# Two more head pairs on the all-fp32 attention path: 40 tiles in place of 32

## The chip, the cores and the metric

The kernel runs on one core of one Trainium2 chip. The metric is the time of one execution on the device in microseconds (us), and the time of the kernel before is the median of three runs. The engines are TensorE (PE in the profile, with its weight loads as PEld), VectorE (DVE), ScalarE (ACT), GpSimd (POOL) and SyncE (SP), which here only issues DMAs. Each takes its instructions in the order of its own program and waits where an operand is not there yet.

## The reference

Attention with a position bias for 4 batches, 8 heads, 576 positions and head dimension 64, then a two-layer network with a gate on the 2304 rows of 512 that come out of it.

```python
scores = scale * np.matmul(q, k.transpose(0, 1, 3, 2))
x = (psi_rel / psi_i)[..., None]                # log1p of distances, over log1p of the row
bias = np.maximum(x @ w1 + b1, 0.0) @ w2        # 32 hidden units, one output per head
scores = scores + bias.transpose(2, 0, 1)[None]
scores = scores - np.max(scores, axis=-1, keepdims=True)
attn = np.exp(scores)
attn = attn / (np.sum(attn, axis=-1, keepdims=True) + 1e-09)
out = np.matmul(attn, v)                        # then [B*S, 512]
h = out @ w_in                                  # 512 -> 2048, weights float64
g = h * np.clip(h + 3.0, 0.0, 6.0) / 6.0
return g @ w_out                                # 2048 -> 512, weights float64
```

## The kernel before

Heads go in pairs (4 to a batch), since two heads of 64 fill 128 partitions. A *unit* is a batch, a head pair and a part of the query rows: part 0 is rows 0 to 255 in four tiles of 128 rows (two row blocks by two heads), part 1 is rows 256 to 575 in five. All 16 units of part 0 come first, batch after batch (units 0 to 15, tiles 0 to 63), then the 16 of part 1. The function `direct` says which units take the direct path; before, those are units 0 to 7, the first two batches.

The direct path of a unit of part 0: the scores of a tile are fp32 products (`qk_step`, L523); DVE adds the bias and finds the maximum (`soft_max`, L555); ACT takes the exponential with the row sum (`soft_exp`, L566); TensorE transposes the tile in five fp32 pieces (`soft_low`, L614) and ACT copies them out of PSUM (L617); `pv_first` multiplies by V in fp32 (L656) and spreads the reciprocals of the row sums over the partitions with four small products (L667); `x_first` scales and splits the result into two fp16 parts (L679 and L685 on ACT, L683 on DVE, L686 on POOL). Since the scaling by the row sum comes last, a tile has no normalisation of its own.

The split path of all other units: q and k are split into a high and a low part (ACT L402, POOL L409), the scores are three products (L543), each tile is normalised by small DVE instructions (L574, L578), split into two fp16 parts (L123 on ACT or L117 on POOL, then L140 on DVE) and transposed by a DMA from SP's queue (L631). V is split too (L123, L140, two small DMAs L452 and L453). The product with V is 28 fp16 matmuls (L698); `x_high` and `x_low` (L712, L140) take the result out.

The network works on a batch part at a time. `ffn` makes `h_ps` (L773), runs ACT L763, DVE L756, ACT L750 and POOL L752 on it, then makes `o_ps` (L796). The weights come as float64 and are converted on the chip: `w_in_prep` and `w_out_prep` take their bit patterns apart on ACT (L256), POOL (L257) and DVE (L264, L267, L270) and split them (L123, L140). At the end of `w_out_prep` the largest power of two over all rows is found by `row_ratio`: a DVE reduction into `m_w` (L146), a TensorE transpose of it (L152), a DVE reduction into `g_w` (L154) and a TensorE product (L156) that spreads the number. Only then can the waiting `g` tiles of batch 0 be scaled (ACT L123, DVE L121) and the first `o_ps` begin.

The bias table is made once in 36 groups of 16 rows (`z_group` on DVE L838 and ACT L842, `bias_mm` on TensorE L855 as 8 matmuls, `bias_out` on ACT L871), stored to DRAM and loaded for each tile pair (L484).

The main loop runs over the tile number n: front(n) takes tile n's maximum, tile n-2's transposes or split, the unit of tile n-5's product with V. Until tile 45 (`open_steady`) a scheduler may reorder instructions on all engines but keeps the data flow; PSUM then holds three double banks for scores, transposes and bias groups (tag `s`) and two single banks for `h_ps`, `o_ps`, `pv_ps` and `m_ps` (tag `w`). From tile 45 on TensorE's order is that of the text, with two double and four single banks.

Of the kernel before, what the change touches and what calls it, by code (L numbers as in the profile page):

```python
# [10 lines left out]
F32 = mybir.dt.float32  # L11
# [4 lines left out]
ALU = mybir.AluOpType  # L16
# [5 lines left out]
PAIRS = H // 2  # L22
# [2 lines left out]
NG = S // 16  # L25
CQ = 2.0 ** -25
VC = 5 * 128
CFG = {'z0': 'AD', 'gz': 12, 'z1': 'AD', 'gz2': 16, 'zeng': 'DDA', 'sg': 'P', 'wm1': 'A', 'wm2': 'RRAAAAAA', 'hl': 'AP', 'gl': 'PP', 'vm': 'A', 'g0': 8, 'rwi': 2.0, 'rw0': 0.3, 'rw1': 0.7, 'ro': 0.85, 'rb': 1.7, 'rf0': 1.3, 'rf': 2.0, 'rf1': 1.55, 'la': 6, 'gq': 2, 'gap': 0.0, 'wu': 8, 'act': 'o', 'g1': 2, 'w64': 5, 'rfo': 2.3, 'tv': 'A', 'pw': 0, 'po': 0, 'gr': 'AD', 'wb': 3, 'fb': 2, 'spn': 45, 'sw': 45, 'ws': 2, 'kn': 10, 'kw': 1, 'os': 11, 'ro2': 2.0, 'bo': 12, 'rb0': 1.5}
F64_BIAS = 2.0 ** -112
F64_MAX = float(np.uint32(0x0FEFFFFF).view(np.float32))  # L30

# [2 lines left out]
def attention_moe_kernel(  # L34
# [16 lines left out]
    nc = tc.nc  # L51
    cfg = CFG
    tc.cur_priority = 10000
    B = qk.shape[0]
    DM, DFF = w_in.shape
    KC = DM // 128
    KF = DFF // 128

    const = ctx.enter_context(tc.tile_pool(name="const", bufs=1))
# [38 lines left out]

    open_psum(stack_p, 3, 2)
    eye_sb = const.tile([128, 128], F32, name="eye_sb")  # L100
    r_sb = const.tile([128, 2, 2 * PAIRS * 4], F32, name="r_sb")
    wi = big.tile([128, 2, KC, DFF], F16, name="wi")
    wo = big.tile([128, 2, KF, DM], F16, name="wo")
    bias_d = [dr_p.tile([H, min(128, S - i), S], F32, name=f"bias{i}") for i in range(0, S, 128)]
# [5 lines left out]
    pscale = {}  # L110
# [270 lines left out]
    def load_direct(b, p):  # L381

        t = qk_p.tile([128, 512 + S], F32, tag="hi", name="qk0")
        with behind():
            dq("q").dma_start(out=t, in_=qkd[b, p])
        qk_t[b, p, 0] = t
# [5 lines left out]
    def load_qk(b, p, u):  # L392
        w = S + QW[u]
        t = st_p.tile([128, 1024], F32, tag="st", name="st")[:, 0:w]
        with behind():
            dq("k").dma_start(out=t, in_=qk[b, p][:, 256 * u:256 * u + w])
        st_t[b, p, u] = t

    def split_qk_a(b, p, u):
        w = S + QW[u]  # L400
        hi = qk_p.tile([128, 512 + S], F32R, tag="hi", name="qkh")[:, 0:w]
        nc.scalar.activation(out=hi, in_=st_t[b, p, u], func=AF.Copy)  # L402
        qk_t[b, p, u] = hi

    def split_qk_b(b, p, u):
        t, hi = st_t[b, p, u], qk_t[b, p, u]
        lo = qk_p.tile([128, 512 + S], F32R, tag="hi", name="qkl")[:, 0:S + QW[u]]
        for c, w in ((KC0[u], S), (QC0[u], QW[u])):
            nc.gpsimd.tensor_sub(  # L409
                out=lo[:, c:c + w], in0=t[:, c:c + w], in1=hi[:, c:c + w].bitcast(F32)  # L410
            )
        qk_t[b, p, u] = (hi, lo)
# [17 lines left out]
    def load_v(b, p, u):  # L430
        if (b, p, u) in v_t:
            return
        if direct(b, p, 4 * u):
            t = v_p.tile([128, VC], F32, tag="vh", name="vf")
        else:
            t = st_p.tile([128, VC], F32, tag="vs", bufs=2, name="vs")
        with behind():
            dq("v").dma_start(out=t, in_=vp[b, p])
        v_t[b, p, u] = t
# [53 lines left out]
    units = [(b, p, u) for u in range(2) for b in range(B) for p in range(PAIRS)]  # L493
# [148 lines left out]
    def x_tile(b, u):  # L642
        if (b, u) not in x_t:
            x_t[b, u] = x_p.tile([128, 2, KC, QW[u]], F16, tag="x", name="x")
        return x_t[b, u]
# [3 lines left out]
    def pv_first(b, p):  # L649
# [20 lines left out]
            )  # L670
        pv_t[b, p, 0] = ps

    def x_first(b, p):
        ps = pv_t.pop((b, p, 0))
        n = 256
        x = x_tile(b, 0)
        xr = hl_p.tile([128, 2, n], F32, tag="hl", name="xr")
        xs, rb = xr[:, 0], xr[:, 1]
        nc.scalar.activation(  # L679
            out=rb, in_=ps[:, 1, 0:n], func=AF.Copy,  # L680
            scale=pscale["x1"][:, p:p + 1] if b else pscale["v0"][1],
        )
        nc.vector.tensor_mul(out=xs, in0=ps[:, 0, 0:n], in1=rb)  # L683
        xh = x[:, 0, p]
        nc.scalar.activation(out=xh, in_=xs, func=AF.Copy)  # L685
        nc.gpsimd.tensor_sub(out=x[:, 1, p], in0=xs, in1=xh)  # L686
# [279 lines left out]
    def aux(n):  # L966
        b, p, t = tiles[n]
        k = unit_no[n]
        l = t - UT[int(t >= 4)][0]
        if l == 0 and PAIRS <= k + 2 < len(units):  # L970
            b2, p2, u2 = units[k + 2]
            if direct(b2, p2, 4 * u2):
                load_direct(b2, p2)
            else:
                load_qk(b2, p2, u2)
        if k + 1 < len(units) and not direct(units[k + 1][0], 0, 4 * units[k + 1][2]):
            if l == 1:
                split_qk_a(*units[k + 1])
            if l == 2:
                split_qk_b(*units[k + 1])  # L980
            if l == 3:
                split_qk_c(*units[k + 1])
        if l == 0 and k < 13:
            load_v(*units[k])
        if l == 1 and 13 <= k + 1 < len(units):
            load_v(*units[k + 1])
        if not direct(b, p, t):
            if l == 2:
                split_v_a(*units[k])
            if l == 3:  # L990
                split_v_b(*units[k])
        if b + 1 < B and t < 4 and p >= 1:
            if b + 1 not in vgen:
                vgen[b + 1] = v_scale(b + 1)
            next(vgen[b + 1], None)
# [28 lines left out]
    for cs in (slice(512, LT), slice(0, 512)):  # L1024
        nc.vector.tensor_scalar(
            out=T[:, cs], in0=T[:, cs], scalar1=w1_sb, scalar2=None, op0=ALU.mult
# [25 lines left out]
    def drain(gen):  # L1052
        for _ in gen:
            pass
# [34 lines left out]
    def open_ffn():  # L1089
        nonlocal phase  # L1090
        drain(gen_w)
        hidden_scale(0)
        for c in range(KC):
            xv = x_t[0, 0][:, :, c]
            nc.vector.tensor_scalar(
                out=xv, in0=xv, scalar1=pscale["r1"][:, c:c + 1], scalar2=None, op0=ALU.mult
            )
        if cfg["fb"] > 1:
            x1 = const.tile([128, KC], F32, name="x1")
            nc.vector.tensor_scalar(  # L1100
                out=x1, in0=pscale["r1"], scalar1=pscale["v1"][1], scalar2=None, op0=ALU.mult
            )
            pscale["x1"] = x1
        stack_a.close()
        del pools["a"], pools["w"]
        pools["g"] = ctx.enter_context(tc.tile_pool(name="g", bufs=1, reuse_waits="tile"))
        pools["f"] = ctx.enter_context(tc.tile_pool(name="f", bufs=2, reuse_waits="tile"))
        queue.append(ffn(0, 0))
        phase = 1
# [36 lines left out]
    for n in range(-1, NT + 7):  # L1146
# [17 lines left out]
        if done is not None and done != (0, 0):  # L1164
            b, u = done
# [20 lines left out]
def _layout(q, k, v, w1, b1, w2, moe_w_in, moe_w_out):  # L1186
# [7 lines left out]
    qkd = _np.concatenate([kd, qd], axis=5).reshape(Bn, PAIRS, 2, 128, HALF + 256)  # L1194
    qkd = qkd.transpose(0, 1, 3, 2, 4).reshape(Bn, PAIRS, 128, 512 + S)[:CFG["fb"]]
    rows = _np.arange(128)[:, None] + 128 * _np.arange(5)[None, :]
# [44 lines left out]
```

## Time and profile before

| | us |
|---|---|
| median of three runs | 698.1 (697.34 to 700.95) |
| the profiled execution | 701.47 |
| its span, from the first to the last instruction | 699.7 |
| TensorE busy | 643.5 |
| ScalarE busy | 488.1 |
| VectorE busy | 481.9 |
| GpSimd busy | 254.5 |

Busy times are unions of an engine's instructions. A matmul's record is longer than the distance to the next, since matmuls are pipelined, so a group is measured from its start to the start of the next group. An fp32 matmul leaves two records in the trace, except the transposes, which leave one; in the program's order it is one row.

### The profile page before, as it was taken

To read this page: it belongs to the slowest core of one execution; us is meant where nothing else is said; L and a number is where in the kernel's file an instruction comes from. 1 tells how busy PE (TensorE), PEld (TensorE's weight loads), DVE (VectorE), ACT (ScalarE), POOL (GpSimd) and SP (SyncE) were. 2 spreads that over 40 slices of the span, in tenths; PEclk is the share of its full clock that TensorE was granted. 3 is DMA by queue.
4 is the path that set the end of the run, shared out by engine and by line. 5 is a ranking of instruction groups with operands and counts; after the bars stand their busy time and mean duration, and the time that the engine had idled before them with its cause. 6 is when DMAs were issued, how large, how long until landed. Compare 5 with 4: busy or idle time off the path is not lost. (4 is left out here: it accounts for less than half of the span.)

```text
span 699.7 us, 15119 instructions
## 1 busy us (share of the span) xinstructions
PE 643.5 (92%) x5558; PEld 456.8 (65%) x5558; DVE 481.9 (69%) x1157; ACT 488.1 (70%) x963; POOL 254.5 (36%) x322
## 2 busy tenths in 40 slices
PE   7687899775999999999898899999999999999998
PEld 2233556552576667688787788767776777777775
DVE  7989868899757786667777877777678767410310
ACT  7987778886657897677668876886678856621620
POOL 1112126774202444045434552565236512410420
PEclk9999999998799999999999999999999999999999
DMA  8899679643798949999999799969796877100000
GB/s 297 298 363 344 242 277 330 217 166 77 218 256 201 246 82 299 189 237 180 244 262 250 142 229 184 219 147 200 139 243 121 161 151 128 21 10 29 1 10 28
DMA packets 175737, 130.13 MB, mean 186 GB/s; under 512 B 137520, under 2 KB 144944, under 8 KB 174640
## 3 DMA queue, kind: packets, MB, share of 16 engines
q1 hardware_dynamic: 165872, 113.84, 65.0%
q10 hardware_dynamic: 9792, 15.34, 7.2%
q8 instruction: 43, 0.70, 0.4%
q14 instruction: 30, 0.25, 0.1%
HBM read 77.24 MB, written 15.34 MB: 132 GB/s over the span
## 5 line engine op out<-in xcount | busy, mean ns | idle before, releaser
L773 PE MATMUL h_ps<-x,wi 128*128 128x256 f16 (+1 forms) x1536 | 200.7, 289 | 15.1 <-DVE xr L683 7.4
L796 PE MATMUL o_ps<-g,wo 128*128 128x256 f16 (+1 forms) x1536 | 195.5, 286 | 1.0 <-ACT g L123 1.0
L773 PEld LDWEIGHTS <-wi 128*128 128x128 f16 x1536 | 148.0, 99 | 63.4 <-issue 21.8
L796 PEld LDWEIGHTS <-wo 128*128 128x128 f16 x1536 | 147.2, 98 | 46.9 <-issue 9.9
L752 POOL TENSOR_TENSOR g<-t,g 128x256 f16<-128x256 f32 (+1 forms) x128 | 100.4, 795 | 127.9 <-ACT g L750 126.9
L566 ACT ACTIVATE bt<-bt,sm 128x576 f32<-128x576 f32 x144 | 110.5, 768 | 51.2 <-DVE sm L555 49.0
L140 DVE SCALAR_TENSOR_TENSOR hl<-bt,sm,hl 128x576 f16<-128x576 f32 x112 | 98.6, 893 | 24.9 <-ACT hl L123 14.3
L756 DVE SCALAR_TENSOR_TENSOR t<-t,t,h_ps 128x320 f32<-128x320 f32 (+1 forms) x112 | 56.3, 515 | 66.3 <-ACT t L763 65.1
L117 POOL TENSOR_SCALAR hl<-bt,sm 128x576 f16<-128x576 f32 x56 | 45.9, 821 | 105.9 <-DVE sm L578 52.6
L750 ACT ACTIVATE g<-t 128x256 f16<-128x256 f32 (+1 forms) x128 | 55.4, 440 | 35.9 <-DVE t L756 35.2
L555 DVE CUSTOM_DVE_ANT_0 bt<-s_ps,bt 128x576 f32<-128x576 f32 x88 | 64.4, 750 | 11.8 <-PE s_ps L543 6.5
L763 ACT ACTIVATE t<-h_ps,t,hr 128x320 f32<-128x320 f32 (+1 forms) x112 | 64.6, 586 | 8.2 <-PE h_ps L773 6.9
L409 POOL TENSOR_TENSOR qkl<-st,qkh 128x576 fp32r<-128x576 f32 (+2 forms) x48 | 57.2, 1214 | 32.0 <-ACT qkh L402 26.5
L855 PE MATMUL b_ps<-z_e,w_sb 128*32 128x288 f32 x448 | 47.6, 445 | 8.5 <-ACT z_e L842 3.3
L806 ACT ACTIVATE ot<-o_ps,os 128x256 f32<-128x256 f32 (+1 forms) x32 | 15.9, 496 | 56.7 <-PE o_ps L796 54.4
L123 ACT ACTIVATE hl<-bt,sm 128x576 f16<-128x576 f32 x56 | 43.0, 769 | 5.3 <-issue 1.2
L574 DVE TENSOR_SCALAR sm<-sm 128x1 f32<-128x1 f32 x112 | 16.8, 150 | 43.2 <-ACT bt L566 42.9
L838 DVE TENSOR_SCALAR z_e<-T,nbp 128x576 f32<-128x576 f32 x69 | 37.4, 586 | 5.4 <-PE b_ps L855 5.2
L543 PE MATMUL s_ps<-qkh 64*128 64x288 f32 x192 | 30.9, 353 | 8.9 <-DVE sm L555 7.3
L842 ACT ACTIVATE z_e<-T,bp 128x576 f32<-128x576 f32 x43 | 32.2, 770 | 6.6 <-PE b_ps L855 2.9
L871 ACT ACTIVATE bo<-b_ps,cv_sb,isc 128x576 f32<-128x576 f32 (+1 forms) x47 | 33.3, 711 | 3.8 <-PE b_ps L855 2.7
L257 POOL TENSOR_SCALAR w<-w 128x1024 f32<-128x1024 f32 x8 | 11.8, 1472 | 63.0 <-ACT wo L256 57.0
(132 smaller groups left out, 891.2 us busy)
## 6 DMA issues: line engine op xcount, KB each, us to landing
bt<-bias SPq DMA_DIRECT2D x36, 576.0 KB, 5.4
bias<-bo ACTq DMA_DIRECT2D x36, 288.0 KB, 5.6
w<-in_w_in_dram SPq DMA_DIRECT2D x8, 1024.0 KB, 7.0
vs<-in_vp_dram SPq DMA_DIRECT2D x24, 320.0 KB, 5.2
st<-in_qk_dram SPq DMA_DIRECT2D x16, 448.0 KB, 4.5
wo<-in_w_out_dram SPq DMA_DIRECT2D x5, 1024.0 KB, 6.6
bt<-bias SPq DMA_DIRECT2D x16, 288.0 KB, 3.5
qk<-in_qkd_dram SPq DMA_DIRECT2D x8, 544.0 KB, 8.7
```

Source lines behind the costliest of these rows:

```text
L117: nc.gpsimd.tensor_scalar(out=out, in0=full, scalar1=scale, scalar2=1.0, op0=ALU.mult, op1=ALU.mult)
L140: nc.vector.scalar_tensor_tensor(out=out, in0=full, scalar=scale, in1=high, op0=ALU.mult, op1=ALU.subtract)
L409: nc.gpsimd.tensor_sub(out=lo[:, c:c + w], in0=t[:, c:c + w], in1=hi[:, c:c + w].bitcast(F32))
L555: nc.vector.tensor_tensor_reduce(out=halves(bt), in0=ps, in1=halves(src), op0=ALU.add, op1=ALU.min, scale=-0.125, scalar=3.0e38, accum_out ...
L566: nc.scalar.activation(out=bt, in_=bt, func=AF.Exp, scale=-1.0, bias=sm[:, 0:1], accum_out=total)
L750: nc.scalar.activation(out=g[:, 0], in_=uu, func=AF.Copy)
L752: e.tensor_sub(out=g[:, 1], in0=uu, in1=g[:, 0])
L756: nc.vector.scalar_tensor_tensor(out=t_t[f], in0=t_t[f], scalar=cols(f)[2], in1=h_t.pop(f)[:, 0:n], op0=ALU.min, op1=ALU.mult,)
L763: nc.scalar.activation(out=t_t[f], in_=h_t[f][:, 0:n], func=AF.Relu, scale=cols(f)[0], bias=cols(f)[1],)
L773: nc.tensor.matmul(out=h_t[f][:, 0:n], lhsT=wi[:, a, c, f * 128:(f + 1) * 128], rhs=x[:, e, c], start=(k == 0), stop=(k == 3 * KC - 1),)
L796: nc.tensor.matmul(out=ops[:, 0:n], lhsT=wo[:, a, f, e * 128:(e + 1) * 128], rhs=g_t[f][:, r], start=(f == 0 and a == 0 and r == 0), stop= ...
L855: nc.tensor.matmul(out=pss[a][32 * k:32 * k + 32, 0:HALF], lhsT=w2_sb, rhs=z[:, a * HALF:(a + 1) * HALF],)
```

## The change

Units 8 and 9, the first two head pairs of the third batch (tiles 32 to 39), take the direct path. `fu` counts the direct units of part 0: 10, where `fb` gave 2 batches of 4. Their q and k are loaded from the second layout (`load_direct`, in place of `load_qk` and its split), V is not split, and the result is scaled in `x_first`. The scale vector, which was made once for batch 1 in `open_ffn`, is made for each batch where it is first needed. `kv` names a number that was written out, with its value kept.

```diff
-CFG = {..., 'fb': 2, ..., 'rb0': 1.5}
+CFG = {..., 'fb': 3, ..., 'rb0': 1.5, 'kv': 13, 'fu': 10}
...
-    r_sb = const.tile([128, 2, 2 * PAIRS * 4], F32, name="r_sb")
+    r_sb = const.tile([128, 2, cfg["fb"] * PAIRS * 4], F32, name="r_sb")
...
     def direct(b, p, t):
-        return b < cfg["fb"] and t < 4
+        return t < 4 and PAIRS * b + p < cfg["fu"]
...
+    def x_scale(b):
+        if f"x{b}" not in pscale:
+            pscale[f"x{b}"] = const.tile([128, KC], F32, name=f"x{b}")
+            nc.vector.tensor_scalar(
+                out=pscale[f"x{b}"], in0=pscale["r1"], scalar1=pscale[f"v{b}"][1], scalar2=None,
+                op0=ALU.mult,
+            )
+        return pscale[f"x{b}"]
...
-            scale=pscale["x1"][:, p:p + 1] if b else pscale["v0"][1],
+            scale=x_scale(b)[:, p:p + 1] if b else pscale["v0"][1],
...
-        if k + 1 < len(units) and not direct(units[k + 1][0], 0, 4 * units[k + 1][2]):
+        if k + 1 < len(units) and not direct(*units[k + 1][:2], 4 * units[k + 1][2]):
...
-        if cfg["fb"] > 1:
-            x1 = const.tile([128, KC], F32, name="x1")
-            nc.vector.tensor_scalar(
-                out=x1, in0=pscale["r1"], scalar1=pscale["v1"][1], scalar2=None, op0=ALU.mult
-            )
-            pscale["x1"] = x1
```

The scheduler orders the instructions before tile 45 anew. The first place is on TensorE, from the end of the output weights' preparation to the product that spreads its scale (`m_ps` with `g_w2`); `pv_ps` is the product with V of unit 7, `b_ps` a bias group, `s_ps` scores, `t_ps` transposes. Before:

```order
L152 MATMUL m_ps_1782<-eye_sb_93,m_w2_1732 1x128
L855 MATMUL b_ps_1846<-z_e_115,w2_sb_104 32x288
L543 MATMUL s_ps_1915<-qkh_1686 128x288 x2
L543 MATMUL s_ps_1915<-qkl_1725,qkh_1686 128x288 x2
L543 MATMUL s_ps_1915<-qkh_1686,qkl_1725 128x288 x2
L543 MATMUL s_ps_1916<-qkh_1686 128x288 x2
L543 MATMUL s_ps_1916<-qkl_1725,qkh_1686 128x288 x2
L543 MATMUL s_ps_1916<-qkh_1686,qkl_1725 128x288 x2
L855 MATMUL b_ps_1846<-z_e_115,w2_sb_104 32x288
L656 MATMUL pv_ps_1819<-atf_1480,vf_1366 64x256 x10
L667 MATMUL pv_ps_1819<-eye_sb_93,r_sb_94 64x128 x3
L156 MATMUL m_ps_1782<-g_w2_1784,ones_sb_102 128x1
```

And in the changed kernel, on the same engine at the same place, where line numbers from L690 on are 9 higher:

```order
L864 MATMUL b_ps_1742<-z_e_115,w2_sb_104 32x288 x2
L523 MATMUL s_ps_1759<-qk0_1364 128x288 x2
L614 MATMUL t_ps_1764<-eye_sb_93,bt_1435 128x128 x5
L152 MATMUL m_ps_1737<-eye_sb_93,m_w2_1703 1x128
L656 MATMUL pv_ps_1778<-atf_1478,vf_1366 64x256 x5
L864 MATMUL b_ps_1742<-z_e_115,w2_sb_104 32x288 x6
L656 MATMUL pv_ps_1778<-atf_1478,vf_1366 64x256 x4
L156 MATMUL m_ps_1737<-g_w2_1739,ones_sb_102 128x1
L656 MATMUL pv_ps_1778<-atf_1478,vf_1366 64x256
L667 MATMUL pv_ps_1778<-eye_sb_93,r_sb_94 64x128 x4
L864 MATMUL b_ps_1805<-z_e_115,w2_sb_104 32x288 x2
L523 MATMUL s_ps_1872<-qk0_1364 128x288 x2
```

The scores of unit 9's second tile pair left the place between the two `m_ps` instructions; nine of the ten products of unit 7 and six bias matmuls stand there now, and the first `o_ps` follows 20 matmuls after the second `m_ps`.

The second place is on VectorE, at the end of the preparation of the output weights, up to the reduction into `m_w2`; `wo` and `cu` are those weights, `hl` the fp16 split of a tile, `vl` that of V, `xr` the result of unit 6. Before:

```order
L140 SCALAR_TENSOR_TENSOR vl_1773<-vs_1604,s_v2_1309,vh_1728 128x640
L270 SCALAR_TENSOR_TENSOR cu_1631<-z_e_115,cu_1631 128x1024
L163 TENSOR_SCALAR w2p_1059<-w2p_1059 128x1
L140 SCALAR_TENSOR_TENSOR hl_1722<-bt_1311,sm_1659,hl_1722 128x576
L140 SCALAR_TENSOR_TENSOR wo_96<-cu_1569,w2s_1060,wo_96 128x1024
L683 TENSOR_TENSOR xr_1653<-pv_ps_1606,xr_1653 128x256
L140 SCALAR_TENSOR_TENSOR hl_1677<-bt_1311,sm_1593,hl_1677 128x576
L838 TENSOR_SCALAR z_e_115<-T_114,nbp_118 128x576
L213 RECIPROCAL w2s_1060<-w2p_1059 128x1
L146 TENSOR_REDUCE m_w2_1732<-w2p_1059 128x1
```

And in the changed kernel, on VectorE at the same place:

```order
L179 TENSOR_REDUCE vparts_1775<-va_1887 128x1
L692 TENSOR_TENSOR xr_1640<-pv_ps_1593,xr_1640 128x256
L140 SCALAR_TENSOR_TENSOR wo_96<-cu_1553,w2s_1058,wo_96 128x1024
L765 SCALAR_TENSOR_TENSOR t_1685<-t_1685,c36_121,h_ps_1621 128x256
L270 SCALAR_TENSOR_TENSOR cu_1618<-z_e_115,cu_1618 128x1024
L163 TENSOR_SCALAR w2p_1057<-w2p_1057 128x1
L765 SCALAR_TENSOR_TENSOR t_1713<-t_1713,c36_121,h_ps_1668 128x256
L847 TENSOR_SCALAR z_e_115<-T_114,nbp_118 128x576
L213 RECIPROCAL w2s_1058<-w2p_1057 128x1
L146 TENSOR_REDUCE m_w2_1703<-w2p_1057 128x1
```

The splits of V and of two tiles are gone from ahead of `m_w2`; two reductions of the next batch's V (one stands just ahead of these rows) and the last two gate instructions moved up into their place, and `xr` comes before the weights' split, not after it.

## Rows read from the trace of the kernel before

**Rows 1.** The page: busy time of each engine, and one of the costliest groups.

```profile
PE 643.5 (92%) x5558; PEld 456.8 (65%) x5558; DVE 481.9 (69%) x1157; ACT 488.1 (70%) x963; POOL 254.5 (36%) x322
...
L555 DVE CUSTOM_DVE_ANT_0 bt<-s_ps,bt 128x576 f32<-128x576 f32 x88 | 64.4, 750 | 11.8 <-PE s_ps L543 6.5
```

**Rows 2.** Busy time by stretch: length, engines (instructions), TensorE clock, DMA share, GB/s.

```profile
129.29:174.15 44.86, 31.32 (x251) 22.23 (x249) 43.88 (x91) 34.25 (x63) 27.56 (x23) 0.90 0.40 123
174.15:188.86 14.71, 12.97 (x80) 6.66 (x76) 9.72 (x33) 9.20 (x17) 4.34 (x6) 0.73 0.72 225
188.86:232.21 43.35, 41.49 (x412) 29.65 (x411) 31.30 (x80) 29.68 (x51) 8.24 (x10) 0.97 0.93 223
232.21:699.70 467.49, 451.32 (x4044) 343.37 (x4040) 288.04 (x700) 308.42 (x657) 180.67 (x251) 1.00 0.71 153
```

**Rows 3.** Timeline of TensorE, direct path: start, us, instruction, shapes, count.

```profile
112.17 2.53 PE L656 MATMUL pv_ps<-atf,vf 128*64 128x256 f32 x20
114.63 0.66 PE L667 MATMUL pv_ps<-eye_sb,r_sb 128*64 128x128 f32 x8
115.22 0.76 PE L523 MATMUL s_ps<-qk 64*128 64x288 f32 x4
115.90 0.77 PE L614 MATMUL t_ps<-eye_sb,bt 128*128 128x128 f32 x5
116.60 0.76 PE L523 MATMUL s_ps<-qk 64*128 64x288 f32 x4
```

**Rows 4.** Timeline of TensorE, split path and bias groups.

```profile
228.99 0.53 PE L543 MATMUL s_ps<-qkh 64*128 64x288 f32 x3 [1.64 <-ACT bo L871]
...
248.17 1.17 PE L698 MATMUL pv_ps<-at,vh 128*64 128x256 f16 x18
...
249.82 1.18 PE L855 MATMUL b_ps<-z_e,w_sb 128*32 128x288 f32 x16
...
253.65 0.54 PE L543 MATMUL s_ps<-qkh 64*128 64x288 f32 x4
...
254.64 1.18 PE L855 MATMUL b_ps<-z_e,w_sb 128*32 128x288 f32 x16
255.75 2.79 PE L773 MATMUL h_ps<-x,wi 128*128 128x256 f16 x24
```

**Rows 5.** Timeline of TensorE ahead of the first `o_ps`; in brackets the wait before.

```profile
169.42 2.72 PE L773 MATMUL h_ps<-x,wi 128*128 128x256 f16 x12 [5.86 <-DVE xr L683]
172.07 2.15 PE L855 MATMUL b_ps<-z_e,w_sb 128*32 128x288 f32 x16
174.15 0.37 PE L152 MATMUL m_ps<-eye_sb,m_w 128*1 128x128 f32 x1
...
179.65 3.65 PE L656 MATMUL pv_ps<-atf,vf 128*64 128x256 f32 x20
...
183.81 0.38 PE L156 MATMUL m_ps<-g_w,ones_sb 1*128 1x1 f32 x2
...
188.86 7.26 PE L796 MATMUL o_ps<-g,wo 128*128 128x256 f16 x65 [1.04 <-ACT g L123]
```

**Rows 6.** Timeline of VectorE at the end of the weights' preparation.

```profile
164.62 1.29 DVE L140 SCALAR_TENSOR_TENSOR vl<-vs,s_v,vh 128x640 f16<-128x640 f32 x1
...
167.04 0.80 DVE L140 SCALAR_TENSOR_TENSOR hl<-bt,sm,hl 128x576 f16<-128x576 f32 x1
...
169.29 0.80 DVE L140 SCALAR_TENSOR_TENSOR hl<-bt,sm,hl 128x576 f16<-128x576 f32 x1
...
170.95 0.14 DVE L146 TENSOR_REDUCE m_w<-w2p 128x1 f32<-128x8 f32 x1
...
173.00 0.47 DVE L756 SCALAR_TENSOR_TENSOR t<-t,c,h_ps 128x256 f32<-128x256 f32 x1
...
175.84 0.27 DVE L154 TENSOR_REDUCE g_w<-m_ps 1x1 f32<-1x128 f32 x1
...
179.37 0.81 DVE L179 TENSOR_REDUCE vparts<-va 128x1 f32<-128x640 f32 x1
```

More of the change, by code (lines that the diff above doesn't have):

```diff
@@ L27 @@
 VC = 5 * 128
-CFG = {'z0': 'AD', 'gz': 12, 'z1': 'AD', 'gz2': 16, 'zeng': 'DDA', 'sg': 'P', 'wm1': 'A', 'wm2': 'RRAAAAAA', 'hl': 'AP', 'gl': 'PP', 'vm': 'A', 'g0': 8, 'rwi': 2.0, 'rw0': 0.3, 'rw1': 0.7, 'ro': 0.85, 'rb': 1.7, 'rf0': 1.3, 'rf': 2.0, 'rf1': 1.55, 'la': 6, 'gq': 2, 'gap': 0.0, 'wu': 8, 'act': 'o', 'g1': 2, 'w64': 5, 'rfo': 2.3, 'tv': 'A', 'pw': 0, 'po': 0, 'gr': 'AD', 'wb': 3, 'fb': 2, 'spn': 45, 'sw': 45, 'ws': 2, 'kn': 10, 'kw': 1, 'os': 11, 'ro2': 2.0, 'bo': 12, 'rb0': 1.5}
+CFG = {'z0': 'AD', 'gz': 12, 'z1': 'AD', 'gz2': 16, 'zeng': 'DDA', 'sg': 'P', 'wm1': 'A', 'wm2': 'RRAAAAAA', 'hl': 'AP', 'gl': 'PP', 'vm': 'A', 'g0': 8, 'rwi': 2.0, 'rw0': 0.3, 'rw1': 0.7, 'ro': 0.85, 'rb': 1.7, 'rf0': 1.3, 'rf': 2.0, 'rf1': 1.55, 'la': 6, 'gq': 2, 'gap': 0.0, 'wu': 8, 'act': 'o', 'g1': 2, 'w64': 5, 'rfo': 2.3, 'tv': 'A', 'pw': 0, 'po': 0, 'gr': 'AD', 'wb': 3, 'fb': 3, 'spn': 45, 'sw': 45, 'ws': 2, 'kn': 10, 'kw': 1, 'os': 11, 'ro2': 2.0, 'bo': 12, 'rb0': 1.5, 'kv': 13, 'fu': 10}
 F64_BIAS = 2.0 ** -112
@@ L982, in aux @@
                 split_qk_c(*units[k + 1])
-        if l == 0 and k < 13:
+        if l == 0 and k < cfg['kv']:
             load_v(*units[k])
-        if l == 1 and 13 <= k + 1 < len(units):
+        if l == 1 and cfg['kv'] <= k + 1 < len(units):
             load_v(*units[k + 1])
```

## Prediction

> **What bounds the kernel now.** I read the page first, then busy time by stretch, then the timelines of TensorE and VectorE in the stretch where units 8 and 9 run. TensorE is busy for 643.5 of 699.7 us [rows 1], so 56 us of waiting are spread over the run, and where they lie decides what more TensorE work costs. From 232.21 us to the end TensorE is busy for 451.32 of 467.49 us [rows 2]: there every added matmul is paid, and only 16.2 us of waits are left. From 129.29 to 174.15 us it is VectorE that is full (43.88 of 44.86 us), while TensorE is busy for 31.32 us at a mean clock of 0.90 [rows 2]. That is the preparation of the output weights: until its scale is known no `o_ps` can begin. The next stretch, 174.15 to 188.86 us, is the chain from the transpose of `m_w` to the first `o_ps`: 14.71 us at a clock of 0.73, VectorE busy for 9.72 us only [rows 2]. The last stretch to look at is 188.86 to 232.21 us, TensorE busy for 41.49 of 43.35 us [rows 2].
>
> So the question has two halves. Added TensorE work before the first `o_ps` falls into waits. Added work after it lengthens the run. Against that stands how much earlier the first `o_ps` comes.
>
> **What a unit costs TensorE.** Direct path, from start to start [rows 3]: scores of a tile 115.22 to 115.90 = 0.68 us, its transposes 0.70, the product with V of a unit 2.46, the spread of the reciprocals 0.59. A unit is 4 x (0.68 + 0.70) + 2.46 + 0.59 = 8.57 us. Split path [rows 4]: scores of a tile pair 253.65 to 254.64 = 0.99, product with V 248.17 to 249.82 = 1.65; a unit is 2 x 0.99 + 1.65 = 3.63 us. Two units are 2 x 4.94 = 9.9 us more.
>
> The rows show two records for an fp32 matmul and one for a transpose, and the 10 products of a unit take 2.46 us [rows 3]. The Trainium skill (FP8 and Floating Point Precision, section TensorE Precision Notes) says that a true fp32 product takes 4 passes through the array. From its figure I estimate, at one column per cycle of the full 2.4 GHz clock and nothing side by side: 0.96 for a tile's scores, 1.07 for its transposes, 4.27 for the product and 0.85 for the spread, 13.2 us for a unit and 19.2 us more for the two; by that the change would lose some 9 us beyond what the rows give. No row bears that out for this case: the measured distances are about 0.65 of it. The sum goes by the rows.
>
> **Where it falls.** I counted the matmuls of the changed program between the same marks. From the tail of the direct tiles (129.29 us) to the transpose of `m_w`, six tiles' scores and four tiles' transposes come in (6 x 0.68 + 4 x 0.70 = 6.9 us), three split tile pairs (3.0) and six bias matmuls (0.8) leave: +3.1 us beside 13.5 us of TensorE waits (44.86 - 31.32). VectorE fills that stretch, so this costs nothing; were that cover gone, 3.1 us. From the transpose of `m_w` to the first `o_ps`: one tile's scores and transposes in, one split pair and two bias matmuls out, +0.1. From the first `o_ps` to the point where the program order is the same again (`h_ps` at 232.21 us): scores of one tile 0.7, transposes of four 2.8, product and spread of units 8 and 9 6.1, and eight bias matmuls 1.1 (a group is 1.11 us, 254.64 to 255.75 [rows 4]) in (one tile's transposes of these stood ahead of the first mark before), two split products (3.3) out: **+7.4 us**, all on the path. Behind that point the order of TensorE's matmuls is the same.
>
> **How much earlier the first `o_ps` comes.** Step one is VectorE's way to `m_w`. Ahead of it leave the split of V 1.29 and two tiles' splits, 0.80 each [rows 6], and one tile's maximum, 0.75 [rows 1], moves behind: 3.64 us. Ahead of it come two reductions of V at 0.81 and two gate instructions at 0.47 [rows 6]: 2.56 us. So `m_w` comes 1.1 us earlier, at 169.85. The small normalisations that leave and the small `r_sb` operations that come about cancel.
>
> Step two is TensorE from there. Before, `m_w` was there at 170.95 [rows 6], and its transpose ran at 174.15, since a bias group of 2.08 us stood ahead [rows 5]. Now two bias matmuls, a tile's scores and its transposes stand ahead: 0.28 + 0.68 + 0.70 = 1.7 us. At the low clock I stretch that by the bias group's own ratio, 2.08 to 1.11: 3.1 us. So the transpose runs between 171.6 and 173.0.
>
> Step three is from the transpose to the product with `g_w`. Before, 9.66 us (174.15 to 183.81 [rows 5]), although `g_w` was there at 175.84 + 0.27 [rows 6]: a split tile pair, two bias matmuls and the whole product of unit 7, 3.58 us at the low clock (179.65 to the next group, of 3.65 [rows 5]), stood in between. Now nine products (2.2 us) and six bias matmuls (0.8): 3.0 us, or 4.8 at the low clock (1.46 and 1.87 times, by the same rows).
>
> Step four is from there to the first `o_ps`, 5.05 us before (183.81 to 188.86, ended by ACT's scaling of g [rows 5]). Now 20 matmuls stand between, 3.3 us by the rows; the scaling still has to run. Between 3.3 and 5.05.
>
> Together the first `o_ps` starts between 177.9 (171.6 + 3.0 + 3.3) and 182.9 (173.0 + 4.8 + 5.1), where it started at 188.86: 11.0 to 6.0 us earlier. I take the middle, 8.4. For the late end speaks that TensorE waited for 5.86 us just ahead and stood at a clock of 0.73 behind [rows 2, 5]; for the early end, that what ended this wait, `xr` on VectorE [rows 5], now stands ahead of the weights' split instead of behind it.
>
> **The sum** is -8.4 + 7.4 = **-1.0 us**. What I cost at nothing: the longer loads of q and k in one layout (SP has no other work there, and the DMA share is 0.40 [rows 2]); ACT's copies of the transposes, which replace its share of the splits (ACT is busy for 34.25 of 44.86 us, so it covers them); eight DMA transposes and four small DMAs of V fewer. These last may help after 188.86 us, where DMAs are busy for 0.93 of the time [rows 2], but the wait that I find there is for ACT's eviction of a bias group (1.64 us [rows 4]). With direct tiles two users of the three double banks become more, so that wait may vanish or come twice: +-1.6 us.
>
> From the profiled execution (span 699.7, with 1.8 us around it 701.47) this gives 700.5; that execution is 3.4 us above the median of the runs shown, so on the median I predict **697.1 us**. The likeliest case has its own range from -11.0 + 7.4 - 1.6 = -5.2 to -6.0 + 7.4 + 1.6 = +3.0: 692.9 to 701.1.
>
> **Rivals.** *The added work is not paid back.* Its place is the first `o_ps`. If it starts less than 7.4 us earlier, that is after 181.5 us, the change loses. One mechanism does it: the product of unit 7 now stands, with the bias matmuls, between the two `m_ps` instructions, and those bias matmuls wait for ReLU pieces from VectorE that queue behind the last weights' split and a tile's maximum. If each of those two costs TensorE its time again (1.29 us like the longest split of [rows 6], and 0.75 for the maximum [rows 1]), and the clock stays low to the end of the chain, the start is at 182.9 + 2.0 = 184.9, and the time 698.1 - 4.0 + 7.4 = 701.5; with the wait for banks doubled, 703.1. For it: the clock of 0.73 [rows 2]. Against it: VectorE has half of that stretch free. I give it 0.21. The skill's four passes would come to the same side at some 9 us more; the rows leave it next to no chance, within these 0.21.
>
> *The whole early end.* Less waiting ahead keeps the clock up, the start comes at 177.9, and the wait for ACT behind it goes with the split tiles: -11.0 + 7.4 - 1.6 = -5.2 us, 692.9 us. For it: the matmuls that now fill the stretch before `m_w`; they stand where TensorE waited. Against it: VectorE still fills that stretch, so TensorE still waits there. I give it 0.31.
>
> *It changes nothing on the path.* Excluded as a case of its own: the program's order shows the matmuls of the direct path after the first `o_ps`, and there TensorE has 1.9 us free in 43.35 [rows 2].
>
> **How the numbers follow.** The likeliest case has 0.48. The measurement tells about 0.5% (3.5 us) from no change, as the three runs lie that far apart. Faster takes the early end and a little of the likeliest, 0.32; slower the first rival and a little, 0.22; the same is 0.46. The range that leaves out two in ten reaches past 692.9 on one side, with some of the last stretch's 16.2 us of waits, to 690, and to the first rival's 703 on the other.
>
> **What would show it.** In the profile after: the first `o_ps` at 178 to 183 us; its distance to the `h_ps` that stood at 232.21 us grown from 43.4 to about 51 us; the length behind that within 1.5 us of 467.5; TensorE's busy time up by 6 to 10 us (less than 9.9 where a higher clock gives some back); `m_w` about 1 us earlier. Wrong would be a first `o_ps` that doesn't move, or a last stretch that changes by more than 3 us, which nothing here explains.

## Result, and the profile after

The changed kernel takes 702.11 us (median of 16 runs, 700.57 to 708.53), the kernel before 699.43 us (16 runs, 696.42 to 701.98). Between the two medians lie 2.7 us. The ratio of the runs, which is not that of the two medians, is 1.0054 with a 95% interval of 1.0037 to 1.0072, that is 3.8 us (2.6 to 5.0): slower, and just beyond the half per cent that I had named as the bound. The forecast was 1.0 us faster, with a range of 690 to 703. The profiled execution took 704.76 us, 2.7 more than its median; the one before, 701.47, is 2.0 above the median of its 16 runs.

The page of the changed kernel, its line of busy times, answers to [rows 1]:

```profile
PE 653.3 (93%) x5582; PEld 458.5 (65%) x5582; DVE 474.5 (67%) x1136; ACT 489.5 (70%) x965; POOL 245.2 (35%) x314
```

TensorE is busy for 9.8 us more, the 9.9 that the rows of the direct and the split path gave for two units. The Trainium skill (FP8 and Floating Point Precision, section TensorE Precision Notes) prices an fp32 product at four passes, from which I had estimated +19.2 us, with nothing running side by side; the trace stays with half of that. Whether that is because there are fewer passes or because products run side by side, this number does not tell.

Busy time by stretch of the changed kernel, cut at the same marks as [rows 2] (the columns are those of that group):

```profile
129.70:172.07 42.37, 32.34 (x242) 21.66 (x240) 40.99 (x81) 33.51 (x63) 22.50 (x21) 0.91 0.44 155
172.07:182.87 10.80, 10.80 (x70) 4.67 (x68) 5.75 (x25) 7.28 (x13) 0.00 (x0) 0.87 0.22 59
182.87:233.88 51.01, 49.21 (x452) 31.77 (x452) 29.94 (x73) 32.70 (x58) 11.34 (x13) 0.99 0.64 175
233.88:703.00 469.12, 454.15 (x4044) 344.81 (x4040) 289.36 (x702) 310.25 (x657) 181.21 (x251) 0.99 0.70 153
```

The first `o_ps` starts at 182.87 us in place of 188.86, 6.0 earlier. The stage behind it lasts 51.01 us in place of 43.35, so the common `h_ps` mark comes 1.67 later. The last stretch is 1.63 longer. Together that is +3.3 us between the two profiled spans, of which the last part may be chance, as is worked out further down. In the second stretch TensorE no longer waits at all: it works for all of 10.80 us, so from the transpose of `m_w` on the start of `o_ps` was set by what stands ahead of it in TensorE's own order.

The timeline of TensorE in the changed kernel, from the wait for unit 6's result into the stage behind the first `o_ps` (answers to [rows 5]; an fp32 matmul leaves two records, so x16 is a whole bias group of 8 matmuls and x2 is one matmul):

```profile
164.36 2.51 PE L782 MATMUL h_ps<-x,wi 128*128 128x256 f16 x12 [2.47 <-DVE xr L692]
168.58 1.18 PE L864 MATMUL b_ps<-z_e,w_sb 128*32 128x288 f32 x4 [1.71 <-POOL g L761]
169.69 1.33 PE L523 MATMUL s_ps<-qk 64*128 64x288 f32 x4
...
172.07 0.42 PE L152 MATMUL m_ps<-eye_sb,m_w 128*1 128x128 f32 x1
172.42 2.70 PE L656 MATMUL pv_ps<-atf,vf 128*64 128x256 f32 x10
175.04 1.17 PE L864 MATMUL b_ps<-z_e,w_sb 128*32 128x288 f32 x12
176.14 1.65 PE L656 MATMUL pv_ps<-atf,vf 128*64 128x256 f32 x8
177.72 0.38 PE L156 MATMUL m_ps<-g_w,ones_sb 1*128 1x1 f32 x2
178.03 0.64 PE L656 MATMUL pv_ps<-atf,vf 64*64 64x256 f32 x2
178.60 0.66 PE L667 MATMUL pv_ps<-eye_sb,r_sb 128*64 128x128 f32 x8
179.19 0.68 PE L864 MATMUL b_ps<-z_e,w_sb 128*32 128x288 f32 x4
179.79 0.76 PE L523 MATMUL s_ps<-qk 64*128 64x288 f32 x4
180.48 0.67 PE L864 MATMUL b_ps<-z_e,w_sb 128*32 128x288 f32 x2
181.08 0.77 PE L614 MATMUL t_ps<-eye_sb,bt 128*128 128x128 f32 x5
181.78 1.16 PE L864 MATMUL b_ps<-z_e,w_sb 128*32 128x288 f32 x10
182.87 3.45 PE L805 MATMUL o_ps<-g,wo 128*128 128x256 f16 x30
186.25 0.67 PE L864 MATMUL b_ps<-z_e,w_sb 128*32 128x288 f32 x2
186.85 0.83 PE L805 MATMUL o_ps<-g,wo 128*128 128x256 f16 x6
...
201.33 1.18 PE L864 MATMUL b_ps<-z_e,w_sb 128*32 128x288 f32 x16
202.44 2.03 PE L805 MATMUL o_ps<-g,wo 128*128 128x256 f16 x17
...
231.32 0.53 PE L543 MATMUL s_ps<-qkh 64*128 64x288 f32 x4 [1.80 <-ACT bo L880]
```

Read the bias matmuls from start to next start. A whole group takes 201.33 to 202.44 = 1.11 us. One matmul alone takes 186.25 to 186.85 = 0.60, two take 179.19 to 179.79 = 0.60, five take 181.78 to 182.87 = 1.09. A group cut into pieces of 2, 1 and 5 takes 2.29 us, twice the price of the whole. The product with V of unit 7 is cut too: four of its products take 176.14 to 177.72 = 1.58 us and the last one 178.03 to 178.60 = 0.57, where by their share of ten in a row (2.46 us [rows 3]) they would take 0.98 and 0.25. Between 179.19 and 182.87 stands one such group, behind the first `o_ps` three more (their last pieces end at 191.41, 197.24 and 220.49). The 5.86 us wait for `xr` of [rows 5] has become 2.47, and the wait for ACT's eviction of a bias group at the stage's end is 1.80 (1.64 in [rows 4]).

The timeline of VectorE in the changed kernel, the two reductions of the scale (answers to [rows 6]):

```profile
168.47 0.14 DVE L146 TENSOR_REDUCE m_w<-w2p 128x1 f32<-128x8 f32 x1
...
172.53 0.28 DVE L154 TENSOR_REDUCE g_w<-m_ps 1x1 f32<-1x128 f32 x1 [0.69 <-PE m_ps L152]
```

`m_w` is there 2.5 us earlier than before, but its transpose starts 3.5 us after it; `g_w` is there at 172.81, but its product starts at 177.72. Both times TensorE is busy with what stands ahead. Up to the end of the first five products with V it works at a low clock: the matmuls from 168.58 to 172.07 take 3.49 us, and the same matmuls take 1.89 (168.97 to 170.86) in the run from tile 36 below, at full clock.

### The profile page after: what moved, and what is told of

It reads as the page before. It is cut to its first block, busy times and chain, and to the rows that moved or that the text cites. A ratio compares the mean times of both kernels' runs of the same rounds, so it can differ in the third digit from the quotient of the medians.

```text
span 703.0 us, 15096 instructions
## 1 busy us (share of the span) xinstructions
PE 653.3 (93%) x5582; PEld 458.5 (65%) x5582; DVE 474.5 (67%) x1136; ACT 489.5 (70%) x965; POOL 245.2 (35%) x314
## 4 chain that ended last, share of the span: by engine, by line
PE 45%; DVE 11%; ACT 6%; issue 5%; DMA 5%; POOL 3%; SPq 1%; ACTq 0%; POOLq 0%; DVEq 0%
PE o_ps L805 22%; PE h_ps L782 11%; PE s_ps L543 4%; PE pv_ps L707 3%; DVE hl L140 3%; DVE t L765 2%; PE b_ps L864 2%; DVE bt L555 2%; ACT bt L566 2%; POOL qkl L409 1%; DMA vs<-in_vp_dram 1%; DVE x L140 1%; DMA bias<-bo 1%; DVE z_e L847 1%; ACT t L772 1%
## 5 line engine op out<-in xcount | busy, mean ns | idle before, releaser
L140 DVE SCALAR_TENSOR_TENSOR hl<-bt,sm,hl 128x576 f16<-128x576 f32 x104 | 92.1, 900 | 23.5 <-ACT hl L123 12.9
L117 POOL TENSOR_SCALAR hl<-bt,sm 128x576 f16<-128x576 f32 x52 | 42.1, 809 | 106.2 <-DVE sm L578 57.6
L409 POOL TENSOR_TENSOR qkl<-st,qkh 128x576 fp32r<-128x576 f32 (+2 forms) x44 | 50.4, 1165 | 25.1 <-ACT qkh L402 21.0
L123 ACT ACTIVATE hl<-bt,sm 128x576 f16<-128x576 f32 x52 | 40.1, 772 | 5.3 <-issue 1.2
L614 PE MATMUL t_ps<-eye_sb,bt 128*128 128x128 f32 x200 | 30.9, 285 | 5.9 <-DVE sm L555 2.9
L864 PEld LDWEIGHTS b_ps<-z_e,w_sb 128*32 128x32 f32 x448 | 15.4, 112 | 29.8 <-issue 7.7
```

The costliest lines, as they stand in the source:

```text
L140: nc.vector.scalar_tensor_tensor(out=out, in0=full, scalar=scale, in1=high, op0=ALU.mult, op1=ALU.subtract)
L409: nc.gpsimd.tensor_sub(out=lo[:, c:c + w], in0=t[:, c:c + w], in1=hi[:, c:c + w].bitcast(F32))
L864: nc.tensor.matmul(out=pss[a][32 * k:32 * k + 32, 0:HALF], lhsT=w2_sb, rhs=z[:, a * HALF:(a + 1) * HALF],)
```

## Experiments

All ratios are to the kernel before, on the same chip. All edits are against the changed kernel. "Text order from tile n" means that TensorE's matmuls are taken out of the scheduler's hand from tile n on and stand in the order of the text; the other engines stay with the scheduler.

**Is added work behind the first `o_ps` paid one to one?** Eight of the ten products with V are left out in units 8 and 9:

```diff
-        for c in range(5):
+        nch = 1 if b == 2 else 5
+        for c in range(nch):
...
-                    start=(c == 0), stop=(c == 4),
+                    start=(c == 0), stop=(c == nch - 1),
```

> The changed kernel with 8 of the 10 fp32 products with V left out in units 8 and 9 (only the first 128 keys count, so the result of these units is another); the order of all other TensorE instructions is the same. It takes 2 x 8 x 0.246 = 3.9 us of TensorE work away, all of it behind the first o_ps. Theory A (what is added behind the first o_ps lies on the path, one to one): 3.9 us less than the changed kernel, so within 1 us of the kernel before, ratio 0.998 to 1.001. Rival B (TensorE waits behind the first o_ps for evictions of bias groups and for banks, so that the work added there is partly hidden and the loss is made of waits): less than 1.5 us is won, ratio 1.003 to 1.006.

Ratio 0.9994 (0.9971 to 1.0016), 699.63 us. The two products with V shrink from 2.46 to 0.48 us each, 4.0 us in all. Its window behind the first `o_ps`:

```profile
182.98:231.06 48.08, 45.50 (x420) 30.25 (x420) 28.70 (x72) 32.48 (x58) 10.00 (x12) 1.00 0.67 183
```

TensorE's busy time in the stage falls by 3.7 us, the stage by 2.9, since 0.8 goes into longer waits, most of it (0.6) into that for ACT's eviction of a bias group. The ratio falls by 0.6%, 4.2 us, with an uncertainty of 2. So TensorE's work there is on the path, nearly one to one; that it were hidden is refuted.

**One unit instead of two**, `'fu': 9`:

```diff
-'fu': 10
+'fu': 9
```

> The changed kernel with unit 8 alone added to the direct path (9 units in place of 10). Counted by kind, TensorE's work behind the first o_ps is 3.2 us more than before instead of 7.4. Theory A (the path gains what the chain to the first o_ps is shortened by and pays what is added behind it): the chain keeps most of its gain, since unit 9's scores are split ones there but no longer ahead of the spread of the scale, so the first o_ps comes 4 to 6 us earlier and the time is 1 to 3 us below before, ratio 0.996 to 0.999. Rival C (each direct unit costs a net amount wherever the chain lies, half of what two cost): 1 to 2 us above before, ratio 1.0015 to 1.003.

Ratio 1.0040 (1.0013 to 1.0067), 700.86 us. Theory A, which counts matmuls, is refuted; rival C's 1.0015 to 1.003 lies inside the interval. The scheduler orders this kernel anew, and again it cuts bias groups. The bias matmuls alone in its stage behind the first `o_ps` (columns: length, TensorE's busy time in them, its weight loads, clock, DMA share, GB/s):

```profile
182.68:232.40 49.72, 13.92 (x129) 4.24 (x128) 0.97 0.86 210
```

As much as with ten units (13.88, below). The run alone does not tell what that costs; the next ones do.

**The scheduler's order against the text's**, for ten units and for eight (`'fu': 8`). The line leaves `open_steady`, which runs at tile 45, and goes into the main loop:

```diff
-        keep_order("PE")
...
+        if n == 33:
+            keep_order("PE")
```

> The changed kernel with TensorE held to the order of the text from tile 33 on instead of tile 45. Bias groups then run whole (8 matmuls in a row) and the two m_ps instructions stand directly behind each other. Theory D (part of the loss is the order that the scheduler found: bias groups cut into pieces of 1, 2 and 5 matmuls cost 0.60 us for a piece of 2 where a whole group of 8 costs 1.11, and the product of unit 7 stands inside the chain): the product with g_w comes 3 to 5 us earlier, the bias groups behind it cost 3 to 4 us less, and the time is 2 to 6 us below that of the changed kernel, ratio 0.997 to 1.002. Rival E (in text order TensorE waits where it could have gone on; the scheduler's order was worth having): 0 to 6 us above the changed kernel, ratio 1.005 to 1.014.

> The same text order from tile 33 on, with 8 direct units as before. It tells the order from the direct path. Theory A plus D: the two effects add, so that this one is below the text order with ten units by the work that the two units add behind the first o_ps, 5 to 8 us less what VectorE is spared, 2 to 6 us: ratio 0.990 to 0.998. Rival E: above before, ratio 1.002 or more. If the direct path is worth having once the order is out of the way, this one is no faster than the text order with ten units.

Ten: 0.9989 (0.9967 to 1.0011), 698.41 us. Eight: 1.0102 (1.0069 to 1.0134), 706.72 us. So the text's order is better than the scheduler's for ten units, as theory D said, and much worse for eight: that the two effects add (0.990 to 0.998) is refuted. In the timeline of the eight units TensorE waits openly for each step of the scale and for the ReLU of a bias group.

```profile
173.87 0.37 PE L152 MATMUL m_ps<-eye_sb,m_w 128*1 128x128 f32 x1 [3.09 <-DVE m_w L146]
176.98 0.58 PE L156 MATMUL m_ps<-g_w,ones_sb 1*128 1x1 f32 x2 [2.73 <-DVE g_w L154]
...
196.67 3.19 PE L864 MATMUL b_ps<-z_e,w_sb 128*32 128x288 f32 x16 [3.89 <-DVE z_e L847]
```

Of these three the ten units have only the one for `g_w`, 1.86 us. From tile 33 the order by itself is no gain; with the direct path it is. But it also moves the chain ahead of the first `o_ps`, so it does not yet show the price of the cuts.

**The cuts alone**: text order from tile 37 (`n == 37`). Up to the first `o_ps` TensorE's matmuls stand as in the changed kernel, behind it the bias groups stand whole.

> The changed kernel with TensorE held to the order of the text from tile 37 on. All that TensorE does up to the first o_ps, and the chain to it, stands as in the changed kernel; behind it, three bias groups that were cut into pieces of 1, 2, 5 or 6 matmuls are whole. Theory D1 (the pieces cost it: three cut groups take 2.3 us each where a whole one takes 1.11): 3.6 us less than the changed kernel, ratio to before 0.999 to 1.002. Theory D2 (what the text order won with ten units was the shorter chain to the first o_ps): no more than 1 us less than the changed kernel, ratio 1.004 to 1.007.

Ratio 0.9976 (0.9949 to 1.0003), 697.96 us. Its windows, and its timeline behind the first `o_ps`:

```profile
171.45:181.16 9.71, 9.71 (x69) 4.28 (x68) 5.74 (x25) 7.26 (x13) 0.00 (x0) 0.97 0.25 66
181.16:229.15 47.99, 44.86 (x452) 31.19 (x452) 28.85 (x72) 32.08 (x58) 9.54 (x12) 1.00 0.71 180
229.15:696.50 467.35, 451.40 (x4044) 342.99 (x4040) 290.45 (x703) 309.79 (x658) 182.56 (x252) 1.00 0.71 154
```

```profile
183.89 1.18 PE L864 MATMUL b_ps<-z_e,w_sb 128*32 128x288 f32 x16
185.00 2.79 PE L805 MATMUL o_ps<-g,wo 128*128 128x256 f16 x24
...
212.38 1.47 PE L805 MATMUL o_ps<-g,wo 128*128 128x256 f16 x12 [1.42 <-ACT ot L815]
```

The bias matmuls alone in that stage, for the kernel before:

```profile
188.86:232.21 43.35, 10.79 (x112) 3.68 (x112) 0.97 0.93 223
```

for the changed kernel:

```profile
182.87:233.88 51.01, 13.88 (x129) 4.08 (x128) 0.99 0.64 175
```

and for this run:

```profile
181.16:229.15 47.99, 9.58 (x129) 3.59 (x128) 1.00 0.71 180
```

The same 452 records stand in the stage as in the changed kernel; TensorE is busy for 4.35 us less, of which 4.30 are the bias matmuls, and 1.3 us come back as waits (a wait of 1.42, for ACT's eviction of an `o_ps`, is new). Of the 4.30 the three cut groups make 3.6 by their price; one more group, the last of the stage, took 1.57 us in the changed kernel and 1.11 here. The stage is 3.0 us shorter. For ten units the cut groups are thus shown as a cost behind the first `o_ps`. The two ratios differ by 5.5 us, with an uncertainty of 2.3. What goes beyond the 3.0 goes with the clock in these two executions: with the same order the chain took 9.71 us at 0.97 against 10.80 at 0.87, and the last stretch 1.8 less at 1.00 against 0.99. Whether whole groups also keep the clock up was not separated.

**The cut ahead of the first `o_ps` too**: text order from tile 36 (`n == 36`).

> The same from tile 36 on: the product with V of unit 7 still stands inside the chain to the scale, but behind the chain one more bias group is whole and scores and transposes of one tile stand behind the first o_ps instead of ahead of it. D1: 1.2 us less than from tile 37 for the group, ratio 0.997 to 1.000. D2: between the changed kernel and the text order from tile 33, ratio 1.001 to 1.004.

Ratio 0.9964 (0.9939 to 0.9989), 698.24 us: faster than both kernels; from the run from tile 37 the ratio does not tell it apart. Its windows, and its timeline of TensorE ahead of the first `o_ps`:

```profile
170.86:177.76 6.90, 6.90 (x62) 3.13 (x59) 4.52 (x19) 4.79 (x9) 0.00 (x0) 1.00 0.21 53
177.76:227.80 50.04, 46.24 (x465) 32.03 (x461) 29.16 (x80) 34.64 (x63) 8.26 (x10) 1.00 0.68 179
```

```profile
168.97 0.68 PE L864 MATMUL b_ps<-z_e,w_sb 128*32 128x288 f32 x4 [1.71 <-issue]
...
170.86 0.27 PE L152 MATMUL m_ps<-eye_sb,m_w 128*1 128x128 f32 x1
171.07 1.51 PE L656 MATMUL pv_ps<-atf,vf 128*64 128x256 f32 x10
172.51 1.16 PE L864 MATMUL b_ps<-z_e,w_sb 128*32 128x288 f32 x12
...
176.65 1.18 PE L864 MATMUL b_ps<-z_e,w_sb 128*32 128x288 f32 x16
177.76 2.79 PE L805 MATMUL o_ps<-g,wo 128*128 128x256 f16 x24
```

The chain is 2.8 us shorter than from tile 37: 1.2 because a group stands whole in place of 2, 1 and 5, and 1.4 because the scores and transposes of a tile moved behind the first `o_ps`, where they are paid (the stage is 2.05 longer). The first `o_ps` starts where I had forecast the early end (177.9 us), but with the scores and transposes of one tile less ahead of it. Here the stretch runs at full clock, and the first five products with V take 171.07 to 172.51 = 1.44 us, in place of 1.23 by count and 2.62 in the changed kernel.

**An earlier hand-over**: text order from tile 25 (`n == 25`).

> Text order on TensorE from tile 25 on, ten direct units: ahead of the scale's product only the places of scores, transposes and hidden layers change. If VectorE sets the time of that stretch, within 1.5 us of the text order from tile 33, ratio 0.997 to 1.001; if TensorE's order there feeds VectorE later, 1 to 4 us above it, ratio 1.000 to 1.005.

Ratio 1.0085 (1.0053 to 1.0117), 705.89 us. From its timeline of TensorE, the product with `g_w`:

```profile
172.94 0.58 PE L156 MATMUL m_ps<-g_w,ones_sb 1*128 1x1 f32 x2 [2.05 <-ACT bt L566]
```

Its product with `g_w` comes 4.8 us ahead of the changed kernel's, and yet the first `o_ps` starts only at 184.61: another 11.7 us of matmuls and waits follow, a part of them at a low clock (the mean from 170.61 to 184.61 us is 0.76). An early scale is no early `o_ps`. The ratio is above what either expectation allowed, and what lengthens the run beyond that start was not followed.

**Eleven units** in text order from tile 33, `'fu': 11`:

> Text order from tile 33 on with 11 direct units. Theory A (the direct path pays in units whose VectorE work lies ahead of the first o_ps and costs its added TensorE work, 4.94 us, where it lies behind): 3 to 6 us above ten units in text order, ratio 1.003 to 1.008. Rival F (each direct unit is worth about 4 us in text order, as the step from eight to ten was): 2 to 5 us below ten units, ratio 0.991 to 0.996.

Ratio 1.0176 (1.0136 to 1.0216), 711.86 us. The sign was right, the size far too small. The trace has one long wait more, which explains part only:

```profile
232.65 0.85 PE L543 MATMUL s_ps<-qkh 64*128 64x288 f32 x3 [4.61 <-ACT bo L880]
```

That profiled execution took 706.55 us, 5 less than the median, so the rest of the loss is not in this trace and stays open. In the trace the loss lies behind the first `o_ps`: 59.4 us to the common `h_ps` mark, where ten units in this order take 50.1.

**What the path is worth in one and the same order**: eight units from tile 36 and from tile 37, nine from tile 36 (`'fu': 8` or `9` with `n == 36` or `37`).

> Eight direct units as before, TensorE in text order from tile 36 on. The split scores of unit 9 and two pieces of bias groups leave the place ahead of the spread of the scale, and the bias groups behind the first o_ps are whole. If what ten units won in this order is the order alone: 1 to 3 us below before, ratio 0.996 to 0.999, so that the direct path of units 8 and 9 adds nothing. If the direct path is worth something in this order (its transposes by TensorE instead of DMA, its maxima earlier): ratio 1.001 to 1.010, as the text order from tile 33 was dear with eight units, and it would wait on VectorE for bias pieces as that one did (3.9 us).

> Eight direct units, TensorE in text order from tile 37 on: up to the first o_ps as before; behind it two bias groups that were cut in two (3 and 5, 1 and 7 matmuls: 0.60 + 1.10 us instead of 1.11) are whole. By the price of the pieces 1.2 us below before, ratio 0.997 to 0.9995. If text order makes TensorE wait for split tiles as it did from tile 33 on: 2 to 6 us above, ratio 1.003 to 1.009.

> Nine direct units, TensorE in text order from tile 36 on. With nine units in the scheduler's order the first o_ps came as early as with ten, and the stretch behind it was 49.7 us where I had counted 46.5: its bias groups were cut into pieces, too. With whole groups: 3 us less than nine units in the scheduler's order (1.004), ratio 0.997 to 1.001. If the time falls with every direct unit in this order: between eight and ten units from tile 36.

| direct units | scheduler's order | text order from 36 | from 37 |
|---|---|---|---|
| 8 | 1 (before) | 1.0076 (1.0050 to 1.0102) | 1.0028 (0.9995 to 1.0061) |
| 9 | 1.0040 (1.0013 to 1.0067) | 1.0026 (0.9993 to 1.0060) | not run |
| 10 | 1.0054 (1.0037 to 1.0072) | 0.9964 (0.9939 to 0.9989) | 0.9976 (0.9949 to 1.0003) |

From tile 36 each unit on the direct path wins about 4 us (1.12% over two, 7.8 us, with an uncertainty of 2.5), from tile 37 about 1.8 (3.6 over two, with an uncertainty of 3.0); in the scheduler's order the two lose 3.8. With eight units the order alone wins nothing: from tile 36 the second reading came true, and from tile 37 the 1.2 us that the price of the pieces promised do not show. So the gain is the path's and the order's together: with the direct path TensorE waits less in that order. The windows and the timeline of eight units from tile 36 show what the two further units save:

```profile
184.04:233.98 49.94, 42.65 (x440) 30.45 (x439) 38.30 (x95) 34.39 (x62) 10.93 (x12) 0.97 0.81 204
```

```profile
170.81 2.72 PE L782 MATMUL h_ps<-x,wi 128*128 128x256 f16 x12 [5.86 <-DVE xr L692]
...
184.04 2.78 PE L805 MATMUL o_ps<-g,wo 128*128 128x256 f16 x24 [2.23 <-ACT g L123]
230.41 0.84 PE L543 MATMUL s_ps<-qkh 64*128 64x288 f32 x3 [2.72 <-ACT bo L880]
```

The stage behind the first `o_ps` is as long with eight units as with ten (49.94 and 50.04 us), though TensorE has 3.6 us less to do in it: it waits for 7.3 us in place of 3.8, 6.2 of them for ACT and 1.1 for VectorE. VectorE is busy for 38.30 us in place of 29.16; whether that holds ACT up was not followed. And the first `o_ps` comes 6.3 us later, with the wait for `xr` that [rows 5] had.

Nine units limit what the price of the pieces explains; their ratio lies above what I expected (0.997 to 1.001), though its interval reaches into it. From tile 36 their bias matmuls in the stage take 11.0 us in place of the 13.9 in the scheduler's order, and TensorE is busy for 43.3 in place of 47.9. Yet the stage is as long, 49.5 us and 49.7, since the waits rise from 1.9 to 6.2. With ten units from tile 37 waits took back only 1.3 of 4.35 us.

## Why the prediction failed

- **TensorE's added work, 9.9 us:** right (9.8), and paid on the path, as the cut product with V showed. The estimate of 19.2 us, four passes with nothing side by side, is refuted.
- **`m_w` 1.1 us earlier:** it came 2.5 earlier. The sign was right, and the other 1.4 us were luck for all that follows. One split of the weights, of which no term of mine spoke, took 2.54 us in the trace before (from 131.61) and 1.28 in the trace after (from 132.27); what else moved I did not follow.
- **The first `o_ps`, 8.4 us earlier. This is the term that failed: measured 6.0.** Its range of 177.9 to 182.9 held (182.87), and so did 171.6 to 173.0 for `m_w`'s transpose (172.07), but both by the luck of the early `m_w`. Taken by themselves all three steps came out above their ranges: from `m_w` to its transpose 3.6 us (forecast 1.7 to 3.1), step three 5.65 (3.0 to 4.8), step four 5.15 (3.3 to 5.05).

  What was wrong in them is the price of the matmuls: I had shared the time of a whole group by their count, 0.14 us for a bias matmul and 0.25 for a product with V, while the program's order leaves them in pieces. At full clock, two bias matmuls ahead of the transpose take 0.60 in place of 0.28, six 1.10 in place of 0.8, and the pieces of 2, 1 and 5 in step four 2.29 in place of 1.1: 1.8 us. The product of unit 7 in pieces of five, four and one takes 1.44 + 1.58 + 0.57 = 3.59 in place of 2.46: 1.1 us. The two `m_ps` matmuls, which I had priced at nothing, take 0.21 and 0.31 at full clock: 0.5 us. Together that is 3.4 us.

  Of these the early `m_w` gave 1.4 back. The low clock took 2.9 us, where the middle of my ranges had left 2.5 for clock and waits; that adds the rest. In the run from tile 37, with the same order up to there, the first `o_ps` came at 181.16: step four was the same 5.15, and the five products took 1.54 in place of 2.62, since the clock had risen earlier (0.97 over the chain in place of 0.87). So 1.7 us of this term differ between two executions.
- **The stage behind, +7.4 us:** +7.66, right in sum and wrong in its parts. The eight bias matmuls more were to cost 1.1; by the source windows bias matmuls cost 3.1 more, since three groups were cut in three, where the kernel before had two cut in two. The rest of the stage gave 1.8 back. The clock there was 0.99 in place of 0.97; how much of it that makes I did not separate.
- **The last stretch, within 1.5 us:** +1.63, a little beyond. One place holds it. In the changed kernel's timeline and window, behind a wait that both kernels have:

```profile
396.63 7.08 PE L782 MATMUL h_ps<-x,wi 128*128 128x256 f16 x48 [1.82 <-DVE x L140]
```

```profile
396.63:403.70 7.07, 7.07 (x50) 5.74 (x51) 4.92 (x14) 5.48 (x13) 3.32 (x5) 0.76 0.77 171
```

and the same in the kernel before:

```profile
394.48 5.42 PE L773 MATMUL h_ps<-x,wi 128*128 128x256 f16 x48 [1.81 <-DVE x L140]
```

```profile
394.48:399.90 5.42, 5.42 (x50) 4.88 (x51) 4.22 (x14) 4.86 (x12) 3.13 (x5) 1.00 0.94 187
```

The same matmuls take 1.65 us longer at a granted clock of 0.76. In one execution each this does not speak for a difference between the kernels: with ten units in text order from 37 and from 36 the last stretch is 467.35 and 467.30 us, as before. So of the +3.3 us between the profiled spans 1.6 may be chance.

Of the rivals, the first came closest: the added work is not paid back because the first `o_ps` starts after 181.5 us. Its place and its condition were right (182.87), its mechanism was not: no split and no maximum on VectorE kept TensorE waiting, TensorE was busy without a gap between the two `m_ps`. That its time, 701.5 us, is near the measured one is luck. The chance of 0.21 was too small for a sum in which a gain and a loss of some 8 us each stood against each other.

With the measured terms the sum up to the common `h_ps` mark is -6.0 + 7.7 = +1.7 us in place of -1.0. The medians differ by 2.7 and the ratio gives 3.8 us; I can't divide what goes beyond the 1.7. The runs bear out the step from the other side: with the same order up to the first `o_ps` and whole groups behind it, the ratio is 0.9976, that is 1.7 us faster (3.6 faster to 0.2 slower), near the 1.0 that I had forecast as if there were no pieces. That nearness is partly luck too, since the pieces ahead of the first `o_ps` still stand in that run.

## What to carry to other kernels

Price a group of small matmuls by the pieces in which the program's order leaves it, not by their count: the order view shows the pieces before anything runs, and the timeline of the kernel before has a row for whole groups and for cut ones. Where a scheduler orders anew, a change and its order are two changes; the same change was worth +3.8 us in the one order and -7.8 in another. A price saved on an engine shortens the run only as far as waits do not take it back, as the nine units showed. Where a gain and a loss of like size make the sum, take neither from the middle of its range without asking which end the program's order supports.

## What the hardware showed that I had not expected

A bias group writes its eight products to two halves of a PSUM double bank, in each to four strips of 32 partitions. One, two or four matmuls in a half cost about the same: 0.60 us for one, 0.60 for two, 1.11 for four and four. The Trainium skill (TensorE: Matmul & The Clock Gate, section Part 3: Packing small matmuls — row/col tiling) says that matmuls in different 32-column tiles of the array run concurrently, so that several last hardly longer than one; the trace agrees, and the pieces count as the halves that they touch. No run here took the strips apart to show it by itself. The product with V behaves alike, in five pairs of two strips of 64: ten products take 2.46 us, one 0.57, five 1.44, about three pairs of the five.

The time of one kernel from run to run goes with the mean granted clock, though not strictly. For the changed kernel the runs at 0.990 took 701.2 to 702.1 us, those at 0.983 703.0 to 705.1, that at 0.978 704.5 and that at 0.971 708.5, but the fastest, 700.6, had 0.987. Behind the same wait of 1.8 us the clock was 1.00 in one execution and 0.76 in another, as the rows above show.
